# A new order for the beginning of a kernel of attention and two expert layers: attention keys earlier, weight keys later, other planner durations

## The chip, the cores and the metric

The kernel runs on one core of a Trainium2 chip. The metric is device microseconds for one execution. The engines are TensorE (PE, with its weight loads shown as PEld), VectorE (DVE), ScalarE (ACT), GpSimd (POOL) and SyncE (SP), which issues all the kernel's own DMAs. Each engine works through its instructions strictly in the order in which the program wrote them.

## The reference

Three stages follow each other; B=4, H=8, S=576, D=64, so there are 2304 tokens of width 512.

```
q_s = softmax(q, axis=-1);  k_s = softmax(k, axis=seq)
x   = q_s @ (k_s^T @ v)                     # linear attention, per batch and head
h   = x @ w_in;  y = (h * clip(h+3, 0, 6) / 6) @ w_out      # 512 -> 2048 -> 512
out = sum_e p_e * (relu(y @ w1[e]) @ w2[e])                 # 4 experts, 512 -> 1024 -> 512
```

`w_in` and `w_out` come as float64 words; the result is float32. Every large product is made with split operands (a high and a low part, three matmuls for one).

## The kernel before, in words

**First layer (h, y).** Tokens are cut into six blocks of 384, the 2048 hidden units into 16 chunks `c` of 128. One *step* is one chunk with one block: `h_part` (L589) makes 12 matmuls of 384 columns (L598 to L600), a gate on ACT, DVE and ACT (L612, L615, L621), a low part on POOL or DVE, and `y_part` another 12 matmuls (L642) into four PSUM banks PS[4] to PS[7]. `PASSES1` (L38) is the order: chunks 0 to 2 on blocks 0, 1, 2 (steps 0 to 8), chunks 3 to 5 on the same blocks (steps 9 to 17), then chunks 0 to 5 on blocks 3 to 5, then the rest. So the first 9 steps need the attention of batches 0 and 1 and three weight chunks, and the chunks 3 to 5 are first needed in step 9.

**Attention.** `k_part` (L379) handles one pair of heads of one batch: a load of k, a maximum on DVE (L412), exp on ACT (L414), five PE transposes (L393), copies out of PSUM (L419, L305 or L307), a product with v (L400) and a normalisation on DVE (L407, L408). `q_part` (L436) does 128 tokens: load, maximum (L457), subtract (L310), exp (L460), sum (L462), reciprocal (L466), multiply (L310), four transposes (L455), a copy (L470). `x_part` (L479) makes x for a segment of tokens: per pair of heads one product (L494), a high part on ACT (L497), a low part on DVE (L501). The first batch may use six PSUM banks for the pieces of its attention (`pa_place`, L375); later batches, and most of the tail of the first, may use two. Block 1 holds the last 192 tokens of batch 0 and the first 192 of batch 1.

**Weights of the first layer.** `w_half` (L534) turns half a chunk (512 float64 words per partition) into a high and a low float32 part. It has a load (L536, 512 KB), four DVE operations (L546, L552, L555, L561), three on ACT (L550, L558, L566) and two on POOL or DVE (L564 and L568, recorded at L310). Four buffers serve the chunks 0 to 2, two serve the later ones.

**Who sets the order.** Nothing of this is written out by hand. `Plan` (L121) is a list scheduler that runs when the program is built. Every operation has an assumed duration per engine; `order` (L150) works back from each step's due time (`START` = 18 for step 0, then one every 24 matmuls) to a due time for each operation, and this is its *key*: on each engine the ready operation with the smallest key goes next (L160 to L162). Main operations (gate, evictions) have far smaller keys and always win; on PE the attention wins over the main matmuls when it is ready; operations that free a PSUM bank get 100 off. `FIRST` (L76) is when the model starts its DMA queue, and before `COLD` it counts PE operations double. An operation that names two engines may land on either. The result is one order of instructions for every engine, SP's loads among them; the chip then keeps that order whatever the real durations are.

Of the kernel before, what the change touches and what calls it, by code (L numbers as in the profile page):

```python
# [72 lines left out]

START, FIRST, COLD = 18.0, 1.65, 30.0  # L76


def hop(a, b):
# [24 lines left out]
    return 0.0131 + 0.4167e-3 * n  # L104


class Op:

    __slots__ = ("eng", "fn", "deps", "key", "take", "give", "start", "end", "place", "on", "n",
                 "place_tile",
                 "left", "at", "then", "due")

    def __init__(self, eng, fn, deps, take, give, key, due):
        self.eng, self.fn, self.deps, self.key, self.due = eng, fn, list(deps), key, due
        self.take, self.give = take, list(give)
        self.start = self.end = self.place = self.on = None


class Plan:  # L121
# [28 lines left out]
    def order(self):  # L150
        for o in self.ops:
            o.left, o.at, o.then = len(o.deps), 0.0, []
        for o in self.ops:
            for d in o.deps:
                d.then.append(o)
        for o in reversed(self.ops):
            if o.due is None:
                e = next(iter(o.eng))
                o.due = min((x.due - self.after(e, x) for x in o.then), default=1e6) - o.eng[e]
            if o.key is None:  # L160
                o.key = o.due - (
                    1e6 if "PE" in o.eng else 1e2 if any(k == "pa" for k, _ in o.give) else 0.0)  # L162
        engines = ("", "SP", "PE", "ACT", "DVE", "Pool")
        clock = dict.fromkeys(engines, 0.0)
        clock["SP"] = FIRST
        cand = {e: [] for e in engines}

        def open_(o):
            for e in o.eng:
                cand[e].append(o)  # L170

        for o in self.ops:
            if not o.left:
                open_(o)
        done, t, total = [], 0.0, len(self.ops)
        while len(done) < total:
            moved = False
            soon = [c for c in clock.values() if c > t]
            for e in engines:
                if clock[e] > t:  # L180
                    continue
                best = None
                for o in cand[e]:
                    lead = self.AHEAD if o.key < 0 else 0.0
                    if o.at > t + lead:
                        soon.append(o.at - lead)
                        continue
                    if best is not None and o.key >= best.key:
                        continue
                    if o.take and self.place_for(o, max(t, o.at)) is None:  # L190
                        continue
                    first = next(iter(o.eng))
                    wait = self.PREFER if first == "Pool" else o.eng[e]
                    if e != first and max(clock[first], t) + o.eng[first] < t + wait:
                        continue
                    best = o
                if best is None:
                    continue
                o = best
                o.start = max(t, o.at)  # L200
                if o.take:
                    x = self.place_for(o, o.start)
                    self.free[o.take[0]].remove(x)
                    o.place = x[0]
                o.on, o.n = e, len(done)
                cold = 2 if e == "PE" and o.start < COLD else 1
                clock[e] = o.start + o.eng[e] * cold
                o.end = clock[e]
                for x in o.eng:
                    cand[x].remove(o)  # L210
                for kind, name in o.give:
                    self.free[kind].append([name.place if isinstance(name, Op) else name() if callable(name) else name, o.end + hop(e, "")])
                    soon.append(o.end + hop(e, ""))
                for x in o.then:
                    x.at = max(x.at, o.end + self.after(e, x))
                    x.left -= 1
                    if not x.left:
                        open_(x)
                done.append(o)
                moved = True  # L220
            if moved:
                continue
            soon += [x[1] for v in self.free.values() for x in v if x[1] > t]
            soon = [x for x in soon if x > t]
            assert soon, "nothing can go on"
            t = min(soon)
        return sorted(done, key=attrgetter("start", "n"))
# [3 lines left out]
def tile_kernel(ctx: ExitStack, tc: tile.TileContext, q, kt, v, w64, w, p, out):  # L231


    nc = tc.nc
# [140 lines left out]
    def pa_place(early):  # L375

        return "pa", None if early else lambda n: n < 2

    def k_part(b, j):  # L379
# [25 lines left out]
        def scale(o):  # L405
# [8 lines left out]
        o2 = add({"ACT": 0.77}, lambda o: nc.scalar.activation(  # L414
            out=t(), in_=t(), func=AF.Exp, bias=nms[ld.place]), [o1])
        to = load("ek", {"": 0.0}, lambda o: None, [o1], ("ek", lambda n: n < 2 or b == 0))
        o3 = add({"PE": 0.43}, lambda o: turn(o, range(4)), [o2, to], pa_place(b == 0))
        o5 = add({"PE": 0.11}, lambda o: turn(o, [4]), [o3], pa_place(b == 0), [("kt", ld)])
        o4 = add({"ACT": 0.6}, lambda o: nc.scalar.activation(  # L419
            out=EK[to.place][:, 0:4 * P], in_=pst[o3], func=AF.Copy), [o3], None, [("pa", o3)])  # L420
        o6 = add({"ACT": 0.26, "DVE": 0.28}, lambda o: copy(
            o, EK[to.place][:D, 4 * P:5 * P], pst[o5][:D, :]), [o5, o4], None, [("pa", o5)])
        o7 = add({"PE": 1.1}, kv, [o6, vld] + bd_readers[j], pa_place(b == 0),
                 [("ek", to), ("v", vld)])
        o8 = add({"DVE": 0.5}, scale, [o7], None, [("pa", o7)])
        kv_done[b, j], kt_last[b, j] = o8, o7
# [9 lines left out]
    def q_part(b, t):  # L436
# [29 lines left out]
        o4 = add({"DVE": 0.18}, lambda o: nc.vector.reciprocal(m(), m()), [o4])  # L466
        o5 = add({"Pool": 1.25, "DVE": 0.7}, lambda o: each(o, ALU.mult), [o4])
        before = [o for s0, s1, bb, o in qt_readers if s0 < t * P + n and s1 > t * P and bb < b]
        o6 = add({"PE": 0.43}, turn, [o5] + before, pa_place(b == 0 and t < 2), [("q", ld)])
        q_done[b, t] = add({"ACT": 0.6}, lambda o: nc.scalar.activation(  # L470
            out=qt[:, :, t * P:t * P + n], in_=pst[o6][:, :, :n], func=AF.Copy),
            [o6], None, [("pa", o6)])
# [54 lines left out]
    def w_part(c):  # L527
        w_done[c], w_place[c] = [], []
        for i in range(2):
            pls = [w_new(w0, (c, i, x)) for x in range(2)]  # L530
            w_place[c] += pls
            w_done[c].append(w_half(c, i, pls))

    def w_half(c, i, space):  # L534
        early = c < PASSES1[0][1]
        ld = load("raw", {"SP": 1.5}, lambda o: nc.sync.dma_start(  # L536
            out=RAW[o.place].bitcast(mybir.dt.int64), in_=w64[c, i]), (),
            ("raw", lambda n: n < 2 or early))

        def word(k, dt):  # L540
            return RAW[ld.place].bitcast(dt).rearrange("p (n t) -> p n t", t=2)[:, :, k]

        def t(dt):
            return WT[o1.place].bitcast(dt)

        o1 = add({"DVE": 0.58}, lambda o: nc.vector.tensor_scalar(  # L546
            out=WT[o.place].bitcast(I32), in0=word(1, I32), scalar1=20, scalar2=0x7FF,
            op0=ALU.logical_shift_right, op1=ALU.bitwise_and), [ld],
            ("wt", lambda n: n < 2 or early))
        o2 = add({"ACT": 0.72}, lambda o: nc.scalar.activation(  # L550
            out=t(I32), in_=t(I32), func=AF.Relu, scale=2.0**23, bias=rebase), [o1])
        o3 = add({"DVE": 0.75}, lambda o: nc.vector.scalar_tensor_tensor(  # L552
            out=t(I32), in0=word(1, I32), scalar=-(2**31), in1=t(I32),
            op0=ALU.bitwise_and, op1=ALU.bitwise_or), [o2])
        o3 = add({"DVE": 0.5}, lambda o: nc.vector.tensor_scalar(  # L555
            out=word(1, I32), in0=word(1, I32), scalar1=0xFFFFF, scalar2=None,
            op0=ALU.bitwise_and), [o3])
        o4 = add({"ACT": 0.68}, lambda o: nc.scalar.activation(  # L558
            out=word(1, F32), in_=word(1, I32), func=AF.Copy, scale=2.0**-20, bias=1.0),
            [o3])  # L560
        o5 = add({"DVE": 0.75}, lambda o: nc.vector.scalar_tensor_tensor(  # L561
            out=word(1, F32), in0=word(0, U32), scalar=2.0**-52, in1=word(1, F32),
            op0=ALU.mult, op1=ALU.add), [o4])
        o6 = add({"Pool": 1.35, "DVE": 0.7}, lambda o: tt(  # L564
            o, t(F32), word(1, F32), t(F32), ALU.mult), [o5], None, [("raw", ld)])
        o7 = add({"ACT": act(DM)}, lambda o: nc.scalar.activation(  # L566
            out=w0[c, i, 0], in_=t(F32), func=AF.Copy), [o6] + space)
        o8 = add({"Pool": 1.35, "DVE": 0.7}, lambda o: half_sub(  # L568
            o, w0[c, i, 1], t(F32), w0[c, i, 0]), [o7], None, [("wt", o1)])
        stage_ops.append(o8)  # L570
        return o8
# [753 lines left out]


    for b in range(B):
        for i in range(SC):
            if i < NPAIR:
                k_part(b, i)  # L1330
            q_part(b, i)
        for s0, n in SEGS[b]:
            x_part(b, s0, n)
    add({"": 0.0}, lambda o: None,
# [157 lines left out]
```

## Time and profile before

| what | value |
|---|---|
| median of three runs | 1240.91 us (1240.31 to 1241.55) |
| the profiled execution | 1242.94 us, span 1241.2 us |
| PE busy | 1200.1 us, 97% of the span |
| DVE busy | 877.5 us, 71% |
| ACT, POOL busy | 595.4 us (48%), 665.4 us (54%) |
| first step's first matmul (L598) | at 34.08 us |
| first matmul on block 1 (step 3) | at 80.52 us |

How to read it: "busy" counts an engine's instructions, and idle time of an engine costs something only where the end hangs on it. PE's busy time also stretches where its clock was granted at the lower of two levels (PEclk below 1.00 in a row is a mean over the stretch). A wait is put down to the semaphore that came last.

### The profile page before, as it was taken

What the parts mean: (1) busy time and instruction counts of PE and PEld (TensorE: products, weight loads), DVE (VectorE), ACT (ScalarE), POOL (GpSimd) and SP (SyncE); (2) the same over time, 40 slices, a digit from 0 to 9 for tenths busy, and PEclk for the clock granted to TensorE, in tenths of its full rate; (3) what the DMA queues carried; (4) which work ended last, traced back from release to release, by engine and by line L of the source; (5) the groups of instructions that cost most, each with busy time, mean ns of one, the idle gap of its engine ahead of it and who ended that gap; (6) DMA issues with size and microseconds to landing.
All of it is one profiled execution on the core that took longest, in us unless ns stands there. A gap on an engine that the chain in (4) does not pass through costs nothing.

```text
span 1241.2 us, 21145 instructions
## 1 busy us (share of the span) xinstructions
PE 1200.1 (97%) x7296; PEld 1151.6 (93%) x7296; DVE 877.5 (71%) x1482; ACT 595.4 (48%) x1257; POOL 665.4 (54%) x659
## 2 busy tenths in 40 slices
PE   4789999999999999999999999999999999999998
PEld 4578999989999999999999989999999999999998
DVE  7989742599884667865555576777777877777775
ACT  5567533565554554544444444444444444444441
POOL 4746324656486775666666643544444554444442
PEclk9889999999999999999999999999999999999999
DMA  8334212344475562455555546877777787777771
GB/s 291 98 129 155 78 69 90 114 155 157 145 230 189 189 244 103 164 185 187 187 187 187 197 159 210 290 248 241 252 248 246 244 288 254 248 247 246 248 249 57
DMA packets 125275, 238.99 MB, mean 193 GB/s; under 512 B 14064, under 2 KB 14064, under 8 KB 125168
## 3 DMA queue, kind: packets, MB, share of 16 engines
q1 hardware_dynamic: 125168, 237.64, 57.6%
q8 instruction: 58, 0.95, 0.3%
q14 instruction: 49, 0.40, 0.1%
HBM read 174.14 MB, written 63.44 MB: 191 GB/s over the span
## 4 chain that ended last, share of the span: by engine, by line
PE 83%; DVE 7%; POOL 3%; issue 3%; DMA 2%; ACT 1%; SPq 0%; POOLq 0%; DVEq 0%; ACTq 0%
PE ps L1249 19%; PE ps L933 18%; PE ps L642 11%; PE ps L1176 11%; PE ps L1054 9%; PE ps L598 4%; PE ps L600 4%; PE ps L599 4%; POOL w L310 1%; PE ps L400 1%; DMA vd<-w 1%; PE ps L494 1%; POOL st L310 1%; POOL g L310 1%; DVE x L310 1%
## 5 line engine op out<-in xcount | busy, mean ns | idle before, releaser
L933 PE MATMUL ps<-x,w 128*128 128x384 f32 x1344 | 264.5, 336 | 0.0
L1249 PE MATMUL ps<-w,g 128*128 128x256 f32 x1737 | 244.4, 283 | 2.0 <-DVE acc L1298 1.8
L1249 PEld LDWEIGHTS ps<-w,g 128*128 128x128 f32 x1737 | 228.6, 190 | 6.0 <-DVE acc L1298 6.0
L642 PE MATMUL ps<-g,w 128*128 128x384 f32 x1152 | 228.1, 343 | 6.0 <-ACT g L621 4.5
L933 PEld LDWEIGHTS ps<-x,w 128*128 128x128 f32 x1344 | 227.3, 189 | 0.8
L642 PEld LDWEIGHTS ps<-g,w 128*128 128x128 f32 x1152 | 200.8, 189 | 13.1 <-ACT g L621 7.1
L1298 DVE SCALAR_TENSOR_TENSOR acc<-ps,pt,acc 128x256 f32<-128x256 f32 x312 | 143.4, 480 | 79.6 <-PE ps L1249 77.6
L310 POOL TENSOR_TENSOR w<-st,w 128x256 fp32r<-128x256 f32 (+1 forms) x129 | 130.7, 1027 | 103.9 <-ACT w L891 70.2
L310 POOL TENSOR_TENSOR g<-t,g 128x384 fp32r<-128x384 f32 x98 | 107.6, 1104 | 116.6 <-ACT g L956 114.4
L1176 PE MATMUL ps<-w,g 128*128 128x512 f32 x576 | 148.9, 394 | 0.0
L599 PE MATMUL ps<-x,w 128*128 128x384 f32 x384 | 129.5, 337 | 2.1 <-DVE x L501 2.0
L1054 PE MATMUL ps<-x,w 128*128 128x384 f32 x672 | 131.0, 335 | 0.0
L598 PE MATMUL ps<-x,w 128*128 128x384 f32 x384 | 130.0, 339 | 0.2 <-ACT x L497 0.2
L600 PE MATMUL ps<-x,w 128*128 128x384 f32 x384 | 129.2, 337 | 0.0
L1054 PEld LDWEIGHTS ps<-x,w 128*128 128x128 f32 x672 | 119.4, 188 | 7.8
L1176 PEld LDWEIGHTS ps<-w,g 128*128 128x128 f32 x576 | 106.8, 188 | 16.5
L615 DVE SCALAR_TENSOR_TENSOR r<-r,ps 128x384 f32<-128x384 f32 x96 | 52.8, 550 | 90.8 <-ACT r L612 90.3
L612 ACT ACTIVATE r<-ps,three 128x384 f32<-128x384 f32 x96 | 55.5, 579 | 111.6 <-PE ps L600 111.5
L956 ACT ACTIVATE g<-t 128x384 fp32r<-128x384 f32 x145 | 73.8, 521 | 43.0 <-DVE t L998 18.0
L310 POOL TENSOR_TENSOR st<-st 128x256 f32<-128x256 f32 (+1 forms) x66 | 71.0, 1081 | 34.2 <-DVE st L561 32.8
L941 ACT ACTIVATE t<-ps 128x384 f32<-128x384 f32 x90 | 44.1, 490 | 70.1 <-PE ps L933 69.9
L599 PEld LDWEIGHTS ps<-x,w 128*128 128x128 f32 x384 | 72.7, 189 | 3.1 <-DVE x L501 3.0
(170 smaller groups left out, 1924.4 us busy)
## 6 DMA issues: line engine op xcount, KB each, us to landing
w<-wd SPq DMA_DIRECT2D x224, 256.0 KB, 3.1
w<-vd SPq DMA_DIRECT2D x224, 256.0 KB, 3.5
vd<-w SPq DMA_DIRECT2D x112, 256.0 KB, 2.3
wd<-w SPq DMA_DIRECT2D x112, 256.0 KB, 2.9
st<-in_w_dram SPq DMA_DIRECT2D x64, 256.0 KB, 3.6
st<-in_w_dram SPq DMA_DIRECT2D x30, 512.0 KB, 3.8
raw<-in_w_dram SPq DMA_DIRECT2D x32, 256.0 KB, 3.4
out_dram<-acc SPq DMA_DIRECT2D x18, 256.0 KB, 2.4
```

The lines of the kernel that those rows point to most:

```text
L310: on(o).tensor_tensor(out=out, in0=a, in1=b, op=op)
L598: nc.tensor.matmul(pst[0], lhsT=hi, rhs=a, start=(k == 0), stop=False)
L599: nc.tensor.matmul(pst[0], lhsT=hi, rhs=b, start=False, stop=False)
L600: nc.tensor.matmul(pst[0], lhsT=lo, rhs=a, start=False, stop=(k == NK - 1))
L612: nc.scalar.activation(out=pst["r"], in_=pst[0], func=AF.Relu, bias=three)
L642: nc.tensor.matmul(y, lhsT=l, rhs=r, start=(s["start"] and not low and m == 0), stop=(s["stop"] and bool(low)))
L933: nc.tensor.matmul(bank(i), lhsT=l, rhs=r, start=(opens and k == 0 and m == 0), stop=(k == 1 and m == 2), skip_group_check=not opens)
L956: nc.scalar.activation(out=made[i][0][:, :n], in_=at(src), func=AF.Relu if raw else AF.Copy)
L1054: nc.tensor.matmul(bank(i), lhsT=l, rhs=r, start=(opens and k == 0 and m == 0), stop=(k == 1 and m == 2), skip_group_check=not opens)
L1176: nc.tensor.matmul(y, lhsT=l, rhs=rr, start=opens and x == 0, stop=closes and x == len(seq) - 1)
L1249: nc.tensor.matmul(y, lhsT=l, rhs=r, start=clears and x == 0, stop=x == len(seq) - 1, skip_group_check=True)
L1298: o1 = add({"DVE": dve(half) + 0.03}, lambda o: nc.vector.scalar_tensor_tensor(out=a, in0=y, scalar=s, in1=a, op0=ALU.mult, op1=ALU.add), ...
```

## The change

No instruction is added or removed, only the numbers that the scheduler orders by. Every operation gets a `bias` that is added to its key: the operations of every weight half get +8.0; those of batch 0's `k_part` and `q_part` get -6.0, those of batch 1's -3.0, those of the batches 2 and 3 nothing. `x_part` and the steps keep their keys. Beside this the assumed durations of several operations change, `FIRST` goes from 1.65 to 0.75, and `COLD` from 30 to 0, so PE operations are no longer counted double at the beginning.

```diff
-START, FIRST, COLD = 18.0, 1.65, 30.0
+START, FIRST, COLD = 18.0, 0.75, 0.0
+WEIGHTS = (8.0,)
+BATCH = (-6.0, -3.0, 0.0, 0.0)
@@ Plan.order
-                o.key = o.due - (
+                o.key = o.due + o.bias - (
                     1e6 if "PE" in o.eng else 1e2 if any(k == "pa" for k, _ in o.give) else 0.0)
@@ k_part
-        o3 = add({"PE": 0.43}, lambda o: turn(o, range(4)), [o2, to], pa_place(b == 0))
-        o5 = add({"PE": 0.11}, lambda o: turn(o, [4]), [o3], pa_place(b == 0), [("kt", ld)])
+        o3 = add({"PE": 0.85}, lambda o: turn(o, range(4)), [o2, to], pa_place(b == 0))
+        o5 = add({"PE": 0.2}, lambda o: turn(o, [4]), [o3], pa_place(b == 0), [("kt", ld)])
-        o7 = add({"PE": 1.1}, kv, [o6, vld] + bd_readers[j], pa_place(b == 0),
+        o7 = add({"PE": 1.2}, kv, [o6, vld] + bd_readers[j], pa_place(b == 0),
@@ q_part
-        o6 = add({"PE": 0.43}, turn, [o5] + before, pa_place(b == 0 and t < 2), [("q", ld)])
+        o6 = add({"PE": 0.8}, turn, [o5] + before, pa_place(b == 0 and t < 2), [("q", ld)])
@@ w_part
+            first = len(plan.ops)
             w_done[c].append(w_half(c, i, pls))
+            for o in plan.ops[first:]:
+                o.bias = WEIGHTS[min(2 * c + i, len(WEIGHTS) - 1)]
@@ w_half (assumed DVE durations of L546, L552, L555, L561)
-        o1 = add({"DVE": 0.58}, lambda o: nc.vector.tensor_scalar(
+        o1 = add({"DVE": 0.6}, lambda o: nc.vector.tensor_scalar(
-        o3 = add({"DVE": 0.75}, lambda o: nc.vector.scalar_tensor_tensor(
+        o3 = add({"DVE": 0.85}, lambda o: nc.vector.scalar_tensor_tensor(
-        o3 = add({"DVE": 0.5}, lambda o: nc.vector.tensor_scalar(
+        o3 = add({"DVE": 0.9}, lambda o: nc.vector.tensor_scalar(
-        o5 = add({"DVE": 0.75}, lambda o: nc.vector.scalar_tensor_tensor(
+        o5 = add({"DVE": 0.95}, lambda o: nc.vector.scalar_tensor_tensor(
@@ the loop over batches
     for b in range(B):
+        first = len(plan.ops)
         for i in range(SC):
             if i < NPAIR:
                 k_part(b, i)
             q_part(b, i)
+        for o in plan.ops[first:]:
+            o.bias = BATCH[b]
         for s0, n in SEGS[b]:
             x_part(b, s0, n)
```

## Rows read from the trace of the kernel before

**Rows 1.** The page: the span, and each engine's busy time.

```profile
span 1241.2 us, 21145 instructions
PE 1200.1 (97%) x7296; PEld 1151.6 (93%) x7296; DVE 877.5 (71%) x1482; ACT 595.4 (48%) x1257; POOL 665.4 (54%) x659
```

**Rows 2.** By stretches: us, busy (x) of PE, PEld, DVE, ACT, POOL; PEclk, DMA, GB/s.

```profile
0.00:78.70 78.70, 49.19 (x248) 40.28 (x248) 66.30 (x123) 45.50 (x96) 45.18 (x44) 0.90 0.56 189
48.00:78.70 30.70, 22.02 (x124) 18.51 (x122) 26.15 (x53) 16.77 (x41) 17.66 (x16) 0.87 0.47 146
78.70:120.30 41.60, 39.86 (x228) 36.68 (x229) 37.41 (x67) 29.08 (x62) 23.90 (x18) 0.93 0.45 144
150.00:200.00 50.00, 50.00 (x286) 48.67 (x285) 20.30 (x39) 19.77 (x44) 18.44 (x23) 1.00 0.21 74
200.00:1241.20 1041.20, 1031.35 (x6338) 996.99 (x6337) 731.31 (x1204) 483.20 (x1018) 568.57 (x569) 1.00 0.61 204
```

**Rows 3.** PE's waits, 0 to 78.7 us: in total, times, longest (the largest).

```profile
PE ps L455 <- ACT qt L470: 4.2, 1, 4.2
PE ps L400 <- DMA vs<-in_v_dram: 4.1, 1, 4.1
PE ps L494 <- DVE x L501: 2.8, 3, 1.5
```

**Rows 4.** DVE's largest wait, 0 to 78.7 us.

```profile
DVE rs L407 <- PE ps L400: 4.8, 3, 2.8
```

**Rows 5.** Instructions in time, PE and DVE: start, us, what.

```profile
34.08 0.45 PE L598 MATMUL ps<-x,w 128*128 128x384 f32 x1 [0.20 <-ACT x L497]
78.39 0.34 DVE L501 TENSOR_TENSOR x<-ps,x 128x192 fp32r<-128x192 f32 x1
80.52 0.69 PE L598 MATMUL ps<-x,w 128*128 128x384 f32 x1
```

**Rows 6.** SP's issues in time: first weight load, first two v loads.

```profile
3.07 0.43 SPq L536 DMA_DIRECT2D st<-in_w_dram  x1
...
6.05 1.02 SPq L383 DMA_DIRECT2D vs<-in_v_dram  x2
```

**Rows 7.** 8.8 to 52.4 us, lines L546, L552, L555, L561: DVE busy (x).

```profile
8.80:52.40 43.60, 3.61 (x6) 0.92 0.53 186
8.80:52.40 43.60, 6.09 (x6) 0.92 0.53 186
8.80:52.40 43.60, 6.68 (x6) 0.92 0.53 186
8.80:52.40 43.60, 6.66 (x6) 0.92 0.53 186
```

**Rows 8.** The same lines there: ns min/median/max, four of the six.

```profile
L546 DVE TENSOR_SCALAR st<-st x4: 416/556/1255, 8.9 to 32.0; 128x512 int32<-128x512 int32 x4
L552 DVE SCALAR_TENSOR_TENSOR st<-st x4: 672/714/1530, 11.4 to 39.4; 128x512 int32<-128x512 int32 x4
L555 DVE TENSOR_SCALAR st<-st x4: 425/1196/2416, 13.0 to 43.5; 128x512 int32<-128x512 int32 x4
L561 DVE SCALAR_TENSOR_TENSOR st<-st x4: 681/1106/1787, 19.1 to 48.8; 128x512 f32<-128x512 uint32 x4
```

**Rows 9.** DVE's groups of instructions, 54.2 to 78.6 us: busy, mean ns.

```profile
L555 DVE TENSOR_SCALAR st<-st 128x512 int32<-128x512 int32 x2 | 2.3, 1126 | 0.0
L457 DVE TENSOR_REDUCE qm<-qs 128x8 f32<-128x512 f32 x2 | 1.3, 672 | 0.0
L1318 DVE TENSOR_TENSOR pt<-pt,sm 128x72 f32<-128x72 f32 x1 | 1.0, 998 | 0.0
```

**Rows 10.** In time, a DVE and two POOL instructions on weights.

```profile
22.82 1.81 POOL L310 TENSOR_TENSOR w<-st,w 128x512 fp32r<-128x512 f32 x1 [1.59 <-ACT w L566]
24.59 1.47 POOL L310 TENSOR_TENSOR st<-st 128x512 f32<-128x512 f32 x1
24.83 1.78 DVE L552 SCALAR_TENSOR_TENSOR acc<-acc 128x512 int32<-128x512 int32 x1
```

More of the change, by code (lines that the diff above doesn't have):

```diff
@@ L112 @@
                  "place_tile",
-                 "left", "at", "then", "due")
+                 "left", "at", "then", "due", "bias")
     def __init__(self, eng, fn, deps, take, give, key, due):
@@ L118, in __init__ @@
         self.start = self.end = self.place = self.on = None
+        self.bias = 0.0
 class Plan:
```

## The prediction, made before the changed kernel ran

> **What bounds the kernel now.** I read the page's busy times first, then a table by stretches, then the waits of PE and DVE up to 80 us, and last the instructions in order of time around the first steps. The page shows a kernel bound by PE: 1200.1 us busy in a span of 1241.2 [rows 1]. So the change, which adds and removes no instruction, can only win or lose the 41.1 us in which PE stands still, and what PE loses at the lower clock. The stretches show where that is: up to 78.7 us PE is busy for 49.19, so it idles 29.5 us; from 78.7 to 120.3 it idles 1.7; from 200 to the end 9.8 in 1041 [rows 2]. Nearly all that an order can win lies before 80 us.
>
> What holds PE there is DVE. It is busy 66.30 of the first 78.7 us, and 26.15 of 30.7 in the last part of it [rows 2]. PE's waits in that stretch are spread thin (the three largest are 4.2, 4.1 and 2.8 us, two on the chain of q, v and x, one on x's low part) [rows 3], which is the look of one late engine and not of one late item. PE becomes dense from the moment block 1 of x is complete: its last low part is written from 78.39 to 78.73, and step 3 opens at 80.52 [rows 5]. From there six steps can run with the three chunks that are already converted. I take the completion of block 1 as the event that the beginning is worth, and ask how much sooner DVE gets there.
>
> **The change part by part.** *Keys.* In the kernel before, chunks 0 to 2 are converted ahead of most of batch 1's attention, since their steps are due at 18 to 26 and block 1 at 30.5. With +8 on the weights and -3 on batch 1, the effective dues are 12 for batch 0's share of block 0, 24.5 for its tail, 26 for chunk 0, 27.5 for batch 1's share of block 1, 30 and 34 for chunks 1 and 2, and 63 for chunk 3. These are the scheduler's numbers and no times; what follows from them is the order. Batch 0 goes first, chunk 0 and batch 1 run side by side, and the gaps that batch 1 leaves (it has two PSUM banks) are filled with chunks 1 and 2. Before, those were already done by then, so the gaps were filled with work that nobody needed yet.
>
> *DVE's work up to block 1.* That filling is the term I can size. Between 54.2 and 78.6 us DVE did chunk 3, needed only in step 9, the shares' normalisation, needed in the second layer, and two maxima of batch 2. Chunk 3 is two halves: the six halves of chunks 0 to 2 took 3.61 + 6.09 + 6.68 + 6.66 = 23.0 us [rows 7], a third is 7.7 (its L555 pair at 2.3 against 6.68/3 = 2.2 agrees [rows 9]). The largest instruction of the shares is 1.0, the two maxima 1.3 [rows 9]. Together 10.0 us that need not stand ahead of block 1, so DVE needs 66.3 - 10.0 = 56.3. Bounds: none of it leaves, if the gaps are filled in the same way (0), or all of it (10.0). I take 10.0, as chunks 1 and 2 now fill these gaps.
>
> *The loads.* SP's order changes too. Before, the first weight load was the sixth issue at 3.07 us, three weight loads (512 KB each) stood ahead of the first v at 6.05 [rows 6], and PE's first product with v then waited 4.1 us [rows 3]; DVE's largest single wait of 2.8 us is the normalisation behind it [rows 4]. Now k, v and q of batch 0 go first as far as their buffers reach, and the weights follow. The 2.8 us of DVE's wait go. DVE's other idle time, 78.7 - 66.3 - 2.8 = 9.6, I keep: most of it is start-up and two banks. Bounds: 0 to 2.8 won, or up to 2.8 lost again if DVE then waits as long for the later weights; I take 2.8 won, since batch 0's attention can run meanwhile.
>
> *The sum at block 1.* 56.3 + 9.6 = 65.9 against 78.7: 12.8 us sooner.
>
> *Contention.* The four DVE operations of a half have minima of 0.416, 0.672, 0.425 and 0.681 and maxima of 1.255, 1.530, 2.416 and 1.787 us in this trace [rows 8]; the long ones run beside a GpSimd operation, as the 1.78 us one at 24.83 does, and the GpSimd operations beside them are long too [rows 10]. Six halves cost 6 x 2.19 = 13.2 us if none meets GpSimd, 6 x 6.99 = 41.9 if each is the longest, and 23.0 as measured. So moving them to other neighbours is worth from -9.9 to +18.9; I take 0, since before as after they share the time with q's subtractions and multiplications.
>
> *What is given back.* The deferred 10.0 us of DVE must still be done. From 78.7 to 120.3 DVE is idle 4.2 [rows 2], so 5.8 do not fit in the stretch that they fall into; from 150 to 200 it idles 29.7 [rows 2]. If batch 2 yields to chunk 3 (93 against 63 in the effective dues), they cost nothing; at worst they cost 5.8. PE's own idle in that stretch is 1.7 with DVE 90% busy, and I take as much again: 1.7.
>
> *PE, clock and either-engine operations.* Assumed PE and DVE durations and `FIRST`, `COLD` change no instruction, only the order that I have just taken; an operation that moves between POOL and DVE is worth about 1 us either way, taken as 0. PEclk averages 0.90 up to 78.7 [rows 2], and a mean between the two levels 1.2 and 2.4 GHz of 0.90 is 15.7 us at the lower one. While DVE sets the end this hardly counts, so 0; bounds 0 to 3 either way.
>
> *Total.* 12.8 - 1.7 = 11.1 us off the profiled execution's 1242.94 (span 1241.2 and 1.7 around it) gives 1231.8. That execution lies 2.0 above the median of the runs, so 1229.8: **1230**. A shift of under 0.2% (2.5 us) counts as no change, about what a measurement of this kernel can tell.
>
> **The rivals.** *Weights late (the gain is small).* Step 0 opens at 34.08 when its x is written [rows 5]. If x is early, chunk 0 decides: before, its first half went from its load's issue at 3.07 [rows 6] to 24.63, the end of the GpSimd operation that starts at 22.82 [rows 10], 21.6 us. Behind seven more loads (about 7 us instead of 3) and just as long on the way it ends near 28.6, so step 0 gains 5.2 us instead of 12.8, and chunks 1 and 2 follow it at that distance. For it: the chain crosses three engines nine times. Against: much of the 21.6 was waiting behind attention, which now is done. 5.2 - 1.7 = 3.5 off: 1237.4.
>
> *No change.* The two banks, not DVE, carry batch 1: then the fillers were free, and block 1 takes as long. DVE's 4.5 us of idle between 48 and 78.7 speak for it; PE's waits on DVE results against it. The 2.8 us of the v wait less 1.7 given back leave 1.1: 1239.8, not to be told from no change.
>
> *Slower: the port.* In this order, batch 1's q operations, half of them on GpSimd, run at the same time as all of chunks 0 to 2. If this lengthens the 24 DVE operations to their maxima, they cost 18.9 more; 12.8 - 18.9 - 1.7 = -7.8, so 1248.7. It decides once the extra is above 11.1, that is a mean of 1.42 us for the 24 against 0.96 now. The Trainium skill, "SBUF — State Buffer", section "SBUF: two separate sides", says that the two engines share a port pair that one of them holds for a whole instruction while the other is fully blocked, which speaks against putting these chains side by side. By that rule a blocked operation grows by the other's length, and the pairs in the trace agree (1.78 against 0.672, beside one of 1.47). For the rival: half of the operations already show it. Against: the reductions, a large part of the attention's DVE work, hardly vary (L457 at 672 ns [rows 9]).
>
> **How the numbers follow.** The forecast has 0.52, with its own range of 1222 to 1235 (contention a third lower on the one side, 5.8 given back on the other). Weights late has 0.20, no change 0.12, slower by the port 0.16. Faster by over 0.2%: 0.52 + 0.17 (weights late, mostly above the bound) + 0.02 = 0.71. Slower: 0.15 from the port and 0.02 from the case without change = 0.17. Within: 0.12. The range goes from 1221 (block 1 at 58, hardly any contention) to 1243; about 0.07 lies below, and 0.13 above, in the port's case.
>
> **What would show it.** Right: the first product with v no longer waits for its load; the last low part of block 1 is written near 66 us; step 3's first matmul is near 67 instead of 80.52; chunk 3's operations and the shares stand behind block 1 on DVE; DVE's sum over chunks 0 to 2 stays near 23; PE's idle after step 3 stays under 4 us up to step 9. Weights late: PE waits before step 0 or 1 for a weight's low part. No change: block 1 still near 78. The port: the 24 operations sum to over 34 us. My forecast is wrong if block 1 is early and PE is then held up in steps 9 to 11 by chunks 3 to 5, or if the order of the later layers, which follows from the same plan, moves by more than these few us.

## The result and the profile after

The changed kernel takes 1226.09 us (median of four, 1225.22 to 1226.93) against 1241.19 for the kernel before in the same measurement: a ratio of 0.9871, 95% interval 0.9859 to 0.9883, that is 15.1 us or 1.3% less. The forecast was 1230 with a range of 1221 to 1243. The span of the profiled execution went from 1241.2 to 1225.2.

The page of the changed kernel, its busy times:

```profile
span 1225.2 us, 21162 instructions
PE 1196.2 (98%) x7296; PEld 1148.9 (94%) x7296; DVE 881.0 (72%) x1486; ACT 596.4 (49%) x1256; POOL 670.7 (55%) x656
```

TensorE has the same 7296 matmuls. Its idle time fell from 41.1 us [rows 1] to 29.0, and its busy time by 3.9. The next two tables cut each execution at the same steps (start of step 3, 18, 30 and 48); columns as in [rows 2]. First the kernel before:

```profile
0.00:80.52 80.52, 50.82 (x256) 41.50 (x257) 68.12 (x124) 46.87 (x98) 46.09 (x44) 0.90 0.56 188
80.52:173.12 92.60, 91.04 (x550) 86.22 (x550) 70.57 (x142) 56.37 (x123) 37.84 (x31) 0.98 0.32 102
173.12:223.04 49.92, 49.92 (x290) 49.92 (x290) 13.91 (x24) 18.33 (x41) 23.67 (x29) 1.00 0.26 91
223.04:303.11 80.07, 77.62 (x433) 74.39 (x433) 67.74 (x100) 45.84 (x92) 49.17 (x46) 1.00 0.40 137
303.11:1241.20 938.09, 930.69 (x5773) 899.56 (x5772) 657.17 (x1095) 427.97 (x907) 508.62 (x510) 1.00 0.64 212
```

and the changed kernel:

```profile
0.00:63.72 63.72, 44.22 (x233) 36.94 (x233) 51.70 (x105) 39.49 (x84) 36.28 (x36) 0.91 0.67 218
63.72:157.62 93.90, 92.75 (x565) 86.50 (x565) 79.58 (x155) 61.56 (x129) 47.91 (x38) 0.99 0.31 100
157.62:210.13 52.51, 52.51 (x298) 51.45 (x298) 15.19 (x28) 19.65 (x42) 23.29 (x29) 1.00 0.25 86
210.13:286.39 76.26, 75.57 (x433) 74.75 (x433) 61.28 (x91) 43.46 (x86) 46.01 (x42) 1.00 0.43 141
286.39:1225.20 938.81, 931.13 (x5773) 899.29 (x5772) 673.25 (x1110) 432.20 (x916) 517.18 (x513) 1.00 0.65 213
```

Step 3 starts 16.8 us earlier, but with fewer matmuls done (233 against 256, part of step 2 among the missing); they come in the next stretches (565 and 298 against 550 and 290). At step 30 the counts of the three stretches agree (1096 in each sum), and there the gain of the beginning is 223.04 - 210.13 = 12.9 us: 10.6 less idle and 2.3 less busy. A second gain of 80.07 - 76.26 = 3.8 lies between steps 30 and 48, far from what the biases touch; the rest gives 0.7 back. 12.9 + 3.8 - 0.7 = 16.0, the difference of the spans.

The changed kernel's instructions in time; the lines answer to L400, L393, L412, L501 and L598 in the kernel before:

```profile
10.11 4.58 PE L405 MATMUL ps<-vs,acc 128*128 128x129 f32 x20 [0.16 <-DMA vs<-in_v_dram]
...
28.20 1.40 DVE L417 TENSOR_REDUCE nm<-acc 128x1 f32<-128x576 f32 x2
...
30.00 0.63 PE L398 MATMUL ps<-ident,acc 128*128 128x128 f32 x4 [1.78 <-DVE x L506]
...
41.73 0.45 PE L606 MATMUL ps<-x,w 128*128 128x384 f32 x1
...
58.95 0.34 DVE L506 TENSOR_TENSOR x<-ps,x 128x192 fp32r<-128x192 f32 x1
...
61.94 0.78 DVE L554 TENSOR_SCALAR st<-st 128x512 int32<-128x512 int32 x1
```

The 4.1 us wait for v [rows 3] is 0.16. Block 1 is complete at 59.29 (L506) instead of 78.73 [rows 5], and chunk 3's first operation (L554 at 61.94) now stands behind it. What I had not looked at before: batch 1's first maximum of k is taken at 28.20 and its first transpose made at 30.00. In the kernel before they were here:

```profile
44.27 0.74 DVE L412 TENSOR_REDUCE nm<-acc 128x1 f32<-128x576 f32 x1
...
47.77 1.03 PE L393 MATMUL ps<-ident,acc 128*128 128x128 f32 x8
```

Its loads of k had been issued by 22.16 there; between them and the maxima VectorE worked mostly on the conversions of chunks 0 to 2. Batch 1's chain, from its first transpose to block 1, takes 31.0 us before and 29.3 after. It starts 17.8 us earlier. Step 0, on the other hand, opens later: at 41.73 instead of 34.08 [rows 5].

Only part of the gain at the beginning lies with batch 1. The next rows split the time up to step 30 at TensorE's first product of x (L494 before, L499 after); what comes ahead of it is batch 0's attention. Before:

```profile
0.00:29.13 29.13, 13.09 (x73) 11.55 (x73) 22.07 (x45) 16.83 (x32) 12.85 (x18) 0.95 0.83 290
29.13:223.04 193.91, 178.69 (x1021) 166.09 (x1022) 130.53 (x244) 104.75 (x228) 94.74 (x86) 0.95 0.33 107
```

and after:

```profile
0.00:23.06 23.06, 12.26 (x72) 10.70 (x72) 16.09 (x39) 12.65 (x26) 9.31 (x16) 1.00 0.88 289
23.06:210.13 187.07, 177.22 (x1021) 164.19 (x1022) 130.37 (x250) 108.06 (x229) 98.18 (x87) 0.96 0.34 113
```

With practically the same number of matmuls in each part, TensorE's idle time falls from 16.0 to 10.8 us in the first part and from 15.2 to 9.9 in the second. Block 0 is complete at 27.68 instead of 38.93.

The four conversion lines of chunks 0 to 2 on VectorE in the changed kernel (the rows that answer to [rows 7], in the same order) sum to 20.0 us against 23.0:

```profile
18.50:59.20 40.70, 5.19 (x6) 0.87 0.62 204
18.50:59.20 40.70, 5.75 (x6) 0.87 0.62 204
18.50:59.20 40.70, 4.38 (x6) 0.87 0.62 204
18.50:59.20 40.70, 4.69 (x6) 0.87 0.62 204
```

### The profile page after: what moved, and what is told of

Its sections match the earlier page's. It is cut to its first block, busy times and chain, and to the rows that moved or that the text cites. A ratio compares the mean times of both kernels' runs of the same rounds, so it can differ in the third digit from the quotient of the medians.

```text
span 1225.2 us, 21162 instructions
## 1 busy us (share of the span) xinstructions
PE 1196.2 (98%) x7296; PEld 1148.9 (94%) x7296; DVE 881.0 (72%) x1486; ACT 596.4 (49%) x1256; POOL 670.7 (55%) x656
## 4 chain that ended last, share of the span: by engine, by line
PE 84%; DVE 5%; POOL 4%; issue 2%; DMA 2%; ACT 1%; SPq 0%; DVEq 0%; POOLq 0%; ACTq 0%
PE ps L1257 19%; PE ps L941 18%; PE ps L650 12%; PE ps L1184 11%; PE ps L1062 10%; PE ps L608 4%; PE ps L607 4%; PE ps L606 4%; POOL w L315 1%; PE ps L405 1%; POOL st L315 1%; DMA st<-in_w_dram 1%; DMA vd<-w 1%; PE ps L499 1%; DVE acc L1306 1%
## 5 line engine op out<-in xcount | busy, mean ns | idle before, releaser
L650 PE MATMUL ps<-g,w 128*128 128x384 f32 x1152 | 225.3, 340 | 1.8 <-ACT g L629 0.8
L315 POOL TENSOR_TENSOR w<-st,w 128x256 fp32r<-128x256 f32 (+1 forms) x133 | 137.3, 1048 | 99.6 <-ACT w L899 59.4
L623 DVE SCALAR_TENSOR_TENSOR r<-r,ps 128x384 f32<-128x384 f32 x96 | 52.6, 549 | 76.5 <-ACT r L620 75.8
L315 POOL TENSOR_TENSOR st<-st 128x256 f32<-128x256 f32 (+1 forms) x56 | 63.2, 1131 | 24.1 <-DVE st L569 20.3
```

The costliest lines, as they stand in the source:

```text
L315: on(o).tensor_tensor(out=out, in0=a, in1=b, op=op)
L650: nc.tensor.matmul(y, lhsT=l, rhs=r, start=(s["start"] and not low and m == 0), stop=(s["stop"] and bool(low)))
```

## The experiments

The theory to test was that VectorE, freed of 10 us of work nobody needed yet, reaches block 1 sooner. Twelve kernels ran, in three groups, each beside the kernel before (medians 1242.03, 1241.36 and 1242.80). The table has, from each one's trace, batch 1's first transpose, block 1 complete, the time between, and the start of step 30; then TensorE's idle time up to its first product of x (idle 1) and from there to step 30 (idle 2); then the median and the ratio to the kernel before. The times of a row come from one execution, and executions of one kernel differ: e4 and e5 spread over more than 5 us, the changed kernel over 1.7.

| run | first transpose | block 1 | chain | step 30 | idle 1 | idle 2 | us | ratio (95%) |
|---|---|---|---|---|---|---|---|---|
| before | 47.8 | 78.7 | 31.0 | 223.0 | 16.0 | 15.2 | 1241.2 | 1 |
| changed | 30.0 | 59.3 | 29.3 | 210.1 | 10.8 | 9.9 | 1226.1 | 0.9871 (0.9859 to 0.9883) |
| e1 biases alone | 29.8 | 69.2 | 39.5 | 210.7 | 11.9 | 10.0 | 1229.7 | 0.9901 (0.9887 to 0.9916) |
| e2 durations alone | 49.1 | 77.0 | 27.9 | 222.5 | 12.7 | 15.6 | 1237.1 | 0.9961 (0.9946 to 0.9975) |
| e3 before, fillers held | 47.3 | 71.8 | 24.6 | 214.7 | 16.2 | 10.3 | 1231.6 | 0.9923 (0.9907 to 0.9940) |
| e4 weight loads early | 28.4 | 62.7 | 34.3 | 220.0 | 9.1 | 17.0 | 1234.2 | 0.9940 (0.9922 to 0.9958) |
| e5 weights later alone | 31.3 | 63.3 | 32.0 | 210.2 | 10.7 | 12.0 | 1228.5 | 0.9898 (0.9877 to 0.9920) |
| e6 batches earlier alone | 45.8 | 70.0 | 24.3 | 210.7 | 8.7 | 12.5 | 1227.1 | 0.9886 (0.9870 to 0.9903) |
| e7 durations, fillers held | 48.2 | 76.5 | 28.3 | 220.3 | 11.8 | 15.1 | 1238.4 | 0.9978 (0.9969 to 0.9987) |
| e8 chunk 0 first | 41.6 | 68.0 | 26.4 | 212.9 | 8.2 | 13.6 | 1230.5 | 0.9909 (0.9894 to 0.9924) |
| e9 batch 1 behind | 50.2 | 71.7 | 21.5 | 215.3 | 10.4 | 16.5 | 1236.0 | 0.9946 (0.9931 to 0.9961) |
| e10 one bank | 33.7 | 80.9 | 47.2 | 232.1 | 10.4 | 25.6 | 1250.9 | 1.0065 (1.0050 to 1.0080) |
| e11 both batches -6 | 34.5 | 65.8 | 31.3 | 208.8 | 8.5 | 12.6 | 1225.8 | 0.9865 (0.9850 to 0.9880) |
| e12 slightly other biases | 31.3 | 57.8 | 26.4 | 213.1 | 10.3 | 14.8 | 1231.4 | 0.9911 (0.9895 to 0.9928) |

**e1, the biases alone** (all assumed durations, FIRST and COLD back):

```diff
-START, FIRST, COLD = 18.0, 0.75, 0.0
+START, FIRST, COLD = 18.0, 1.65, 30.0      # and the eight durations of the diff
```

Expected: 

> Only the biases of the change, with the assumed durations, FIRST and COLD of the kernel before. Theory A (the order by the biases frees VectorE ahead of block 1): nearly all of the 15.1 us, 1226 to 1230 us, block 1 complete near 60 us. Rival B (the planner's better durations do it, by orders that the real durations then keep): only a small part, 1237 to 1241 us, block 1 complete after 70 us.

12.3 us of the gain, at the upper end of A's range; block 1 came later than A said (69.2). At step 30 it is as far ahead as the changed kernel (12.3 against 12.9) although its block 1 is some 10 us later, so the completion of block 1 is not what the lead hangs on.

**e2, the durations alone:**

```diff
-WEIGHTS = (8.0,)
-BATCH = (-6.0, -3.0, 0.0, 0.0)
+WEIGHTS = (0.0,)
+BATCH = (0.0, 0.0, 0.0, 0.0)
```

Expected: 

> Only the assumed durations, FIRST and COLD of the change; all biases 0. Theory A: little, 1236 to 1241 us, since the weights of chunks 0 to 2 still stand ahead of batch 1. Rival B: most of the gain, 1226 to 1231 us.

4.9 us, A's range, but not where I had looked: step 30 starts 0.5 us earlier than in the kernel before, and steps 30 to 48 take 76.08 instead of 80.07. In the kernel before, the gate's operation on VectorE (L615) stands there behind conversions that the planner had priced at 0.7 to 0.75 us. VectorE's operations there:

```profile
240.81 1.56 DVE L561 SCALAR_TENSOR_TENSOR st<-st 128x512 f32<-128x512 uint32 x1
242.41 1.39 DVE L310 TENSOR_TENSOR st<-st 128x512 f32<-128x512 f32 x1
243.73 1.83 DVE L310 TENSOR_TENSOR w<-st,w 128x512 fp32r<-128x512 f32 x2
245.48 0.54 DVE L615 SCALAR_TENSOR_TENSOR r<-r,ps 128x384 f32<-128x384 f32 x1
```

TensorE's waits between 240 and 268 us that hang on such gates, and the longest of them with what led to it:

```profile
PE ps L642 <- ACT g L621: 2.0, 4, 0.9
```
```profile
254.33 1.79 DVE L561 SCALAR_TENSOR_TENSOR st<-st 128x512 f32<-128x512 uint32 x1 [0.15 <-ACT st L558]
256.04 0.54 DVE L615 SCALAR_TENSOR_TENSOR r<-r,ps 128x384 f32<-128x384 f32 x1
256.67 0.52 ACT L621 ACTIVATE g<-r 128x384 fp32r<-128x384 f32 x1 [0.84 <-DVE r L615]
257.25 2.38 PE L642 MATMUL ps<-g,w 128*128 128x384 f32 x12 [0.86 <-ACT g L621]
```

In the changed kernel no wait on ACT's g is left between steps 30 and 48. Of its 3.8 us there, 1.8 are idle time and 1.8 busy time of the products that read g (217 matmuls take 42.5 us before and 40.7 after). In this order the durations alone bring the second gain, but they are not the only way to it: e3 has it with the old durations, and e12 has most of it missing with the new ones. The two parts nearly add up: 12.3 + 4.9 = 17.2 against 15.1 together.

**e3, the kernel before with the fillers held:**

```diff
         ld = load("raw", {"SP": 1.5}, lambda o: nc.sync.dma_start(
-            out=RAW[o.place].bitcast(mybir.dt.int64), in_=w64[c, i]), (),
+            out=RAW[o.place].bitcast(mybir.dt.int64), in_=w64[c, i]), () if early else x_done[1],
-        ld = add({"SP": 0.6}, lambda o: nc.sync.dma_start(out=pt, in_=p))
+        ld = add({"SP": 0.6}, lambda o: nc.sync.dma_start(out=pt, in_=p), x_done[1])
```

Expected: 

> The kernel before, with one thing added to the plan: the loads of chunks 3 and later, and of the shares, come after block 1 is complete, so that their VectorE work cannot fill gaps ahead of it. Theory A's largest term taken alone (10.0 us of fillers on VectorE): block 1 complete near 69 us instead of 78.7, 1231 to 1234 us. Rival C (the gaps are left by the two PSUM banks, and fillers in them were free): block 1 still at 75 to 79 us, 1238 to 1242 us.

By the time alone this was theory A's number: 10.5 us less. Block 1 came 6.9 us earlier, not 9.7, and 4.3 of the 12.1 us by which its span is shorter lie between steps 30 and 48 (75.76), where nothing was held. In this order the fillers did stand in the way. In the kernel before, a high part of x was ready at 74.65, and its low part (L501) waited on VectorE behind a conversion of chunk 3 (L555):

```profile
74.32 0.33 ACT L497 ACTIVATE x<-ps 128x192 fp32r<-128x192 f32 x1 [0.15 <-PE ps L494]
74.42 1.47 DVE L555 TENSOR_SCALAR st<-st 128x512 int32<-128x512 int32 x1
75.81 0.34 DVE L501 TENSOR_TENSOR x<-ps,x 128x192 fp32r<-128x192 f32 x1
```

I took it for half a confirmation; e7 shows that it doesn't carry over to another order.

**e4, the weight loads early, the conversions late:**

```diff
-                o.bias = WEIGHTS[min(2 * c + i, len(WEIGHTS) - 1)]
+                o.bias = 0.0 if "SP" in o.eng else WEIGHTS[min(2 * c + i, len(WEIGHTS) - 1)]
```

Expected: 

> The changed kernel, but the weight loads on SyncE's queue get no bias and go out early again, ahead of v; the conversion keeps its +8. Theory A (VectorE's order is what counts): within 2 us of the changed kernel, 1225 to 1228 us. Rival D (the gain comes from v's loads no longer standing behind the weights): the 4.1 us wait of TensorE for v is back and with it 3 to 4 us, 1229 to 1231 us.

Neither. It is 8 us behind the changed kernel, but not by the mechanism of D: two v loads still went out ahead of the first weight load, and TensorE's first wait for v was 0.3 us. In step 2 it waits 2.8 us for a weight's low part and later 1.9 for v of batch 3, and TensorE's mean granted clock up to step 3 is 0.85 against 0.91. Up to step 30, e4 first, then the changed kernel:

```profile
0.00:220.02 220.02, 193.91 (x1092) 178.03 (x1093) 150.86 (x288) 120.48 (x257) 107.18 (x105) 0.95 0.40 132
0.00:210.13 210.13, 189.48 (x1093) 174.89 (x1094) 146.46 (x288) 120.70 (x255) 107.49 (x102) 0.97 0.40 132
```

For the same matmuls e4 idles 5.5 us more and is busy 4.4 us more, at a lower mean granted clock. This execution was the slowest of its four (1237.47), so it shows more than the 8 us of the medians.

**e5 and e6, the biases one at a time** (with the new durations): `BATCH` all 0, and `WEIGHTS` 0.

Expected of e5: 

> The change's durations and +8 on the weights, no bias on the batches. Theory A (what counts is that chunks 0 to 2 fall behind batch 1 on VectorE): +8 moves chunk 1 from 22 to 30 against block 1 at 30.5, so nearly the whole change, 1226 to 1229 us, block 1 at 59 to 64 us. Rival E (the early batches' own bias does it): 1233 to 1237 us, as with the durations alone.

Expected of e6: 

> The change's durations and -6 and -3 on the batches 0 and 1, no bias on the weights. Theory A: batch 1's share of block 1 moves only from 30.5 to 27.5, still behind chunks 0 to 2 at 18 to 26, so little over the durations alone: 1233 to 1237 us. Rival E: 1226 to 1230 us.

Each alone brings nearly the whole change: 12.9 us and 14.3. e5 goes as A said. e6 does not, its time is rival E's: batch 1 starts at 45.8, nearly as late as before, block 1 comes at 70.0, and yet its step 30 is 12.3 us ahead. There the chain is short (24.3 us) and step 0 opens at 26.32. More of its gain lies with batch 0: TensorE idles 8.7 us up to the first product of x (16.0 before, 10.8 changed). An early batch 1 is a way to the gain, not the only one.

**e7, the durations with the fillers held** (the edit of e3 on e2's kernel).

Expected: 

> The change's durations, no bias, but chunk 3 and later and the shares held (in the plan) until block 1 is complete. If the fillers are the one thing that the biases take off VectorE's path, the two together give the whole change: 1225 to 1229 us. Rival (the place of chunks 0 to 2 relative to batch 1 has a worth of its own): 1230 to 1234 us.

Above both ranges, and against theory A: in this order its largest term is worth next to nothing. The held chunk 3 stands at 83.66, well behind block 1, and block 1 is still at 76.5: 0.5 us earlier than in e2, and the kernel is no faster (1238.4 against 1237.1). VectorE in e7, the end of block 1 and the first held operation:

```profile
76.17 0.36 DVE L506 TENSOR_TENSOR x<-ps,x 128x192 fp32r<-128x192 f32 x1
...
83.66 1.29 DVE L554 TENSOR_SCALAR st<-st 128x512 int32<-128x512 int32 x1
```

and the engines over its chain of batch 1 (28.3 us):

```profile
48.20:76.50 28.30, 22.16 (x129) 18.34 (x128) 23.80 (x54) 18.20 (x43) 13.83 (x13) 0.86 0.46 140
```

VectorE is busy 84% of it (86% in e2, with chunk 3): other work that could wait fills the gaps. Mostly it costs the chain nothing, but not always. Here a maximum for batch 2's q (L462) waits for its load, and batch 1's last normalisation (L412), whose product (L405) had ended at 69.17, stands behind it; TensorE then waits 2.03 us:

```profile
67.89 1.28 PE L405 MATMUL ps<-vs,acc 128*128 128x129 f32 x10
70.34 0.69 DVE L462 TENSOR_REDUCE qm<-qs 128x8 f32<-128x512 f32 x1 [2.36 <-DMA qs<-in_q_dram]
70.94 0.16 DVE L412 RECIPROCAL rs<-ps 128x1 f32<-128x1 f32 x1
71.64 0.63 PE L460 MATMUL ps<-ident,spare 128*128 128x128 f32 x4 [2.03 <-DVE bd L413]
```

e2 has such a wait too, of 1.19 us. So fillers are not free as such: it depends on what stands right behind them.

**e8, chunk 0 first:** `WEIGHTS = (0.0, 0.0, 8.0)`.

Expected: 

> The changed kernel with bias 0 instead of 8 on the two halves of chunk 0, so that step 0, which opens at 41.7 us in the changed kernel and at 34.1 in the kernel before, opens early again. Theory A (VectorE's sum up to block 1 decides, not the start of step 0): step 0 opens near 30, block 1 stays within 2 us of 59, 1224 to 1228 us. Rival F (TensorE's 14 us between block 0 and step 0 are lost time): 1218 to 1223 us.

Step 0 opens at 25.85 as meant, but the kernel is 4 us slower than the changed one, above both ranges: batch 1's first transpose waits until 41.6 and block 1 until 68.0. F's gain does not appear, nor in e11, whose step 0 opens at 26.85 and which equals the changed kernel. Batch 1 started later in both (41.6 and 34.5 against 30.0), so no run prices an early step 0 by itself.

**e9, batch 1 behind the weights, batch 0 ahead:** `BATCH = (-6.0, 8.0, 0.0, 0.0)`.

Expected: 

> The changed kernel with batch 1 at +8 instead of -3, so that it stands behind the chunks 0 to 2 again as in the kernel before, while batch 0 stays ahead of everything. So far batch 1's first transpose came at 28 to 49 us and block 1 some 24 to 34 us after it (39 in one run), whatever filled the gaps. Theory G (the gain is that this chain over two PSUM banks starts earlier): first transpose at 43 to 50, block 1 at 70 to 78, 1233 to 1239 us. Rival H (batch 0's early place and its loads carry the gain): 1226 to 1230 us.

Theory G's time and block 1; the first transpose, at 50.2, just misses its range. Of the changed kernel's 15 us, 8 to 9 go when batch 1 alone is put back. The rows up to step 30, split at the first product of x, show which:

```profile
0.00:22.02 22.02, 11.61 (x73) 10.05 (x73) 16.05 (x39) 12.64 (x26) 9.31 (x16) 1.00 0.91 316
22.02:215.32 193.30, 176.77 (x1021) 162.44 (x1022) 136.60 (x253) 108.98 (x233) 94.22 (x86) 0.97 0.36 114
```

The first part keeps its gain (10.4 us idle, 10.8 in the changed kernel); the second has lost it (16.5, against 9.9 changed and 15.2 before).

**e10, one PSUM bank for the later batches:**

```diff
-        return "pa", None if early else lambda n: n < 2
+        return "pa", None if early else lambda n: n < 1
```

Expected: 

> The changed kernel with one PSUM bank instead of two for the attention of the later batches (and the tail of batch 0). Theory G (the two banks set the 29 us of batch 1's chain): the chain takes 45 us or more, block 1 after 75 us, 1238 to 1255 us. The prediction's view (VectorE's sum up to block 1 sets it): the chain stretches by less than 6 us, 1226 to 1232 us.

Theory G's ranges, all three: the chain goes from 29.3 to 47.2 us and the kernel is slower than before the change. The engines over that chain, and two of TensorE's three largest waits up to 110 us (the largest, 6.3, is mostly the one before the first transpose of all):

```profile
33.70:80.90 47.20, 32.62 (x154) 27.26 (x154) 42.35 (x71) 26.66 (x54) 31.56 (x22) 0.83 0.42 129
```
```profile
PE ps L398 <- DVE x L506: 6.2, 2, 5.0
PE ps L499 <- DVE x L506: 5.9, 4, 2.1
```

TensorE's transposes and products wait for the x operation that empties the bank. VectorE is busy 90% of this stretch too, though it is 18 us longer than with two banks: its busy share does not tell whether it sets the pace. The edit also holds the batches 2 and 3 to one bank (step 30 is 22 us late), so the 25 us are not all batch 1's.

**e11, both batches at -6, weights at 0; e12, slightly other biases** (`WEIGHTS` 7, `BATCH` -5 and -2.5).

Expected of e11: 

> The change's durations, batches 0 and 1 both at -6, weights at 0: between the run with only the batches' biases (batch 1 three units ahead) and the one with only the weights' (eight). Theory G: batch 1's first transpose between 31 and 46 us; 1225 to 1229 us, perhaps below both kernels, since step 0 opens near 27. Rival (each such order is luck of some 5 us either way): anywhere from 1224 to 1236 us.

Expected of e12: 

> The changed kernel with its biases slightly other: +7 for the weights, -5 and -2.5 for the batches. If the gain belongs to the order that the biases stand for: 1225 to 1229 us. If much of it is the luck of one list schedule: more than 3 us away from 1226.

e11 equals the changed kernel (intervals 0.9850 to 0.9880 and 0.9859 to 0.9883); no run shows a version clearly better. e12 is the warning: block 1 is complete even earlier (57.8), and yet it is slower than the changed kernel by 4 to 5 us (0.9911 against 0.9871, intervals apart). Step 2 waits 3.7 us for a weight's low part instead of 1.8, step 30 is 3.0 late, and steps 30 to 48 take 78.8 instead of 76.3.

## Why the prediction was right, and where it was not

*Time and sign.* Right: 15.1 us less where 11.1 was forecast. But part of the agreement is luck. Block 1 came 19.4 us sooner and not 12.8, and of this 6.5 were given back by step 30 and not 1.7: two errors that nearly cancel. The forecast put all of the gain into the beginning, where 12.9 lie; another 3.8 lie between steps 30 and 48. The new durations bring them alone (e2; e3 has them with the old ones), and I had costed the durations at nothing beyond the order at the start. That step failed. An order of the later layers that moves by more than a few us was among the prediction's own signs of being wrong.

*What bounds the beginning.* The step that named DVE as the engine that holds PE was not shown by the rows it used. It stood on VectorE's 26.15 of 30.7 us busy [rows 2], and on PE's waits; but [rows 3] leaves out the largest, 7.0 us in two waits on ACT (L414), 5.9 of it before the first transpose. e7 and e10 have shares like it, 84% and 90%, at chains of 28.3 and 47.2 us. The two PSUM banks, which the rival without change named, are part of what paces batch 1: with one bank its chain took 47.2 us (e10). They don't set it alone, for with two it took from 21.5 us (e9) to 39.5 (e1), with VectorE 95% busy in both. The rival's conclusion was wrong because the chain moved forward as a whole.

*The marker.* Block 1's completion is not what the beginning is worth. It came 9.5 us sooner in e1 and 8.7 in e6, and step 30 came 12.3 sooner in both; it came 16.0 sooner in e4 and 20.9 in e12, and step 30 only 3.0 and 9.9.

*The fillers, 10.0 us.* They did go behind block 1, as foretold. Taking them away alone was worth next to nothing in e7's order, the lower bound of 0; in e3's order block 1 came 6.9 us sooner. No run prices them in the changed order. What the runs show in their place are two things of about equal size. Batch 0's attention is done sooner, which takes 5.2 us from TensorE's idle time up to the first product of x. And batch 1's chain starts 17.8 us earlier, because its maxima of k no longer queue behind the conversions of chunks 0 to 2; behind the first product of x another 5.4 us of idle time go, and e9, with batch 1 put back, loses these and keeps the 5.2.

*The loads, 2.8 us.* The wait for v went, as forecast; it lies in batch 0's part. Its share was not measured alone: e4, meant for it, left v in front.

*Contention, 0.* 23.0 became 20.0, 3 us to the good. The port rival asked for more than 34 to be right; in sum the conversions beside batch 1's GpSimd work did not get longer, though one of the four lines did (3.61 to 5.19). The pair that the rival read in [rows 10] agrees only roughly: the operation grew by 1.1 us beside one of 1.47, of which 1.23 were left when it began.

*Given back, 1.7.* Measured from step 3 to step 30: 16.8 became 12.9. The 3.9 are no stalls but work: TensorE idles 0.4 us from step 3 to step 9 (my bound was 4), and has 23 matmuls more to do in the later stretches, which were missing at step 3. Step 3 was a poor marker too, as it can start before step 2 is finished.

*Weights late.* Step 0 is late by 7.7 us, where that rival had it early by 5.2 (its own figures, 34.08 less 28.6, give 5.5). The wait for a weight's low part is there, 1.8 us, but in step 2 and not before steps 0 or 1. The late step 0 seems to cost little, as TensorE does batch 1's attention meanwhile: e8 and e11, with an early one, are no faster.

*Open.* What decides the idle time behind the first product of x is shown only in part. An early batch 1 is not enough: e4 and e12 start it at 28.4 and 31.3 and idle 17.0 and 14.8 us there, as much as the kernel before. Nor is it needed: e3 starts it at 47.3 and idles 10.3. Small changes of the biases shuffle the whole list, and some 5 us either way follow that I can place (steps 30 to 48, one wait in step 2, a lower granted clock) but not foresee.

## What to carry to other kernels

A busy engine in front of a starved one is not its bound until you know that its work is needed: look for the chain that the late result waits on, with its buffers, and ask when that chain starts. Check the event by which you measure a gain, too: here block 1's completion and the time won went apart. In a static order, work that can wait does harm where something critical stands right behind it, the more so if it is itself late, as the maximum that waited for its load in e7; and a planner's too small duration can be paid where a short critical operation queues behind it, perhaps 200 us from where one looks. When one order gains, try a neighbour of it: here slightly other numbers moved the time by 5 us, a third of the gain.

## What the runs showed of the hardware

Nothing that I had not expected, except in size: two operations on 128 x 512 elements, which the planner had priced at 0.7 to 0.75 us, took 1.39 and 1.56 on VectorE around 241 us, as long as those in the crowded beginning.
